# Top-32 mask in a fused attention and MoE kernel: from a compare-multiply-sum on VectorE to a parametric ReLU and an exponential on ScalarE

## The chip, the cores and the metric

The kernel runs on one core of a Trainium2 chip. The metric is the device time of one execution in microseconds (us). Five engines work beside each other, each through its own instructions in a fixed order: PE (matrix multiplication, with its weight loads shown as PEld), DVE (vector), ACT (scalar, activation functions), POOL (GpSimd) and SP (which only issues DMAs here). An engine waits at an instruction until what it needs is there, and everything behind it on that engine waits too.

## The reference

Three layers are computed one after the other, all in float32:

```python
# 1. attention, batch 4, heads 8, sequence 576, head size 64
scores = scale * q @ k.T                       # scale = 1/8
kth = partition(scores, -32)[..., -32]         # the 32nd largest of a row
scores = where(scores >= kth, scores, -1e9)
attn = exp(scores - max(scores))
attn = attn / (sum(attn) + 1e-9)
x = attn @ v                                   # -> 2304 tokens x 512
# 2. h = x @ w_in (512 x 2048);  g = h * cos(h);  x = g @ w_out
# 3. gate: softmax of x @ w_gate (8 experts), 8 Sinkhorn rounds over all tokens
#    out = sum over experts e of P[:, e] * (relu(x @ w1[e]) @ w2[e])   (512 x 1024 x 512 each)
```

## The kernel before

Precision: most products are made of three matmuls on halves ("hi" and "lo") of the float32 operands. ACT makes the hi half as a rounded copy (`split_cols`, L345), POOL or DVE the lo half by a subtraction (L347). Matmuls of that kind stand on lines L372 to L374 and L383 to L387.

Attention works on tiles of 128 query rows by 576 keys. `att_tile` (from L436) makes one of them: PE computes the scores in two halves of 288 columns into one PSUM bank `s` (L447, L448; L451 in the first tiles), ACT copies each half to `sc` (L457). DVE finds the 32 largest values of each row by four MAX8 (L459, L465; each gives eight values, kept in `m`) with three MATCH_REPLACE8 between them (L464), which strike out what was found. The largest value is in column 0 of `m`, the 32nd in column 31. Beside that chain ACT makes the exponentials of all 576 scores (L461), with minus an eighth of the largest value as bias (POOL, L460). When the 32nd value is there, DVE makes one pass (L466) that compares each score with it, multiplies the exponential by the 0 or 1 and sums the row. POOL adds 1e-9 (L468), DVE takes the reciprocal (L469), POOL scales the row (L470), PE turns the tile over by five transposes into PSUM bank `t` (L475), and ACT and DVE split it there into hi and lo (L493, L494). `att_out` (L501 to L509) multiplies by v.

There are 144 such tiles. The first 24 (three query tiles of eight heads, `attention_tile`) come at the start, beside the decoding of the weights `w_in` and `w_out`; they feed the second layer of the first 384 tokens (`moe1_tile_a`, `moe1_tile_b`, L631 to L671). The other 120 (`attention`) come after it. Beside these, PE has filler work: the expert products of the first 384 tokens (`fill(e, 0, LEAD)`, matmuls of 384 and 512 columns), one part of the second layer (`moe1`), and the expert products of the next 512 tokens (`fill(e, LEAD, 4)`). What is left of filler work when attention ends is done after it, then come three more parts of the second layer, the Sinkhorn rounds, and the dense expert products of the remaining tokens.

The order on each engine is not written by hand. `Plan.add` records each operation with its engine, a planned duration and what it reads and writes; `Plan.issue` then walks through a planned time and on each engine takes the ready operation of the best class (`PRIORITY`: on PE attention goes before the filler), and emits the instructions in that order. The planned durations are the second argument of `put`. Changing an operation or its planned duration therefore moves instructions on all engines. Tiles overlap through rings of buffers: four `sc`, two `wk`, three `ex`, four `m`; the PSUM banks `s` and `t` exist once.

Of the kernel before, what the change touches and what calls it, by code (L numbers as in the profile page):

```python
# [14 lines left out]
AF = mybir.ActivationFunctionType  # L15
ALU = mybir.AluOpType
# [5 lines left out]
MAGIC = 12582912.0  # L22
HALF_PI = 1.5707963267948966
LOWEST = -3.0e38


CLASSES = ("first attention", "first mlp", "decode", "attention", "mlp")
# [43 lines left out]
class Plan:  # L71
# [32 lines left out]
    def add(self, eng, cost, emit, reads=(), writes=(), prio=0.0, func=None, nbytes=0):  # L104
        op = Op()
        op.eng, op.cost, op.emit, op.func, op.bytes = eng, cost, emit, func, nbytes
        k = len(self.ops)
        op.prio = (prio, k)
        deps = set()

        def norm(acc):
            for a in acc:
                if isinstance(a, tuple) and isinstance(a[0], View):
                    b, lo, _ = a[0].span
                    yield b, lo + a[1], lo + a[2]
                elif isinstance(a, View):
                    yield a.span
                elif isinstance(a, Buf):
                    yield a, 0, 1 << 30
                else:  # L120
                    yield a

        pools = set()
        for b, lo, hi in norm(reads):
            pools.add(b.pool)
            for l, h, i, wr in b.log:
                if wr and l < hi and lo < h:
                    deps.add(i)
        for b, lo, hi in norm(writes):
            pools.add(b.pool)  # L130
            for l, h, i, wr in b.log:
                if l < hi and lo < h:
                    deps.add(i)
        for b, lo, hi in norm(writes):
            b.log = [e for e in b.log if not (lo <= e[0] and e[1] <= hi)]
            b.log.append((lo, hi, k, True))
        for b, lo, hi in norm(reads):
            b.log.append((lo, hi, k, False))
        for p in pools:
            for old in self.pools[p].get("after", ()):  # L140
                deps.update(self.users.get(old, ()))
                self.users[p + "<"] = True
        for p in pools:
            self.users.setdefault(p, []).append(k)
        deps.discard(k)
        op.deps = deps
        self.ops.append(op)
        return k
# [65 lines left out]
def mm_ns(n):  # L214
    return max(107.0, n / 2.4 + 3.0)


def act_ns(n, psum=False, ap=False):
    return (51.0 if psum else 93.0) + n / 1.2 + (93.0 if ap else 0.0)


def dve_ns(n, fast=False):
    return 66.0 + n * (0.53 if fast else 1.042)
# [6 lines left out]
def fused_kernel(tc, kq, vv, w_in, w_out, w_gate, w1, w2, out, B=4):  # L230
# [4 lines left out]
    V, A_, G_, T_ = nc.vector, nc.scalar, nc.gpsimd, nc.tensor  # L235
    H, S, D = 8, 576, 64
# [25 lines left out]
    def put(eng, cost, emit, reads=(), writes=(), func=None, nbytes=0):  # L262
        return add(eng, cost, emit, reads, writes, PRIORITY[eng][CLASSES.index(work)], func, nbytes)
# [172 lines left out]
    def att_tile(stats, dests, plain=None):  # L436

        at_f = plain and plain["at"]  # L440
        sc, m, wk, ex = sc_r(), m_r(), wk_r(), ex_r()
        for c in (slice(0, 288), slice(288, 576)):
            o = lambda: ps_s.ap[:, 0:288]

            def qk(c=c):
                for i, (q, c0, hd) in enumerate(stats):
                    T_.matmul(o(), q.ap[:, c0 : c0 + 128], hd["kh"].ap[:, c], start=i == 0, stop=False)  # L447
                    T_.matmul(o(), q.ap[:, c0 : c0 + 128], hd["kl"].ap[:, c], start=False, stop=i == len(stats) - 1)  # L448

            def qk_plain(c=c):  # L450
                T_.matmul(o(), plain["q"].ap[:, plain["h"], :], plain["k"].ap[:, plain["h"] % 2, c], start=True, stop=True)  # L451

            if plain:
                put("PE", 4 * mm_ns(288), qk_plain, [plain["q"], plain["k"]], [ps_s])
            else:
                put("PE", 2 * len(stats) * mm_ns(288), qk, [x for q, _, hd in stats for x in (q, hd["kh"], hd["kl"])], [ps_s])
            put("ACT", act_ns(288, psum=True), lambda c=c: A_.activation(sc.ap[:, c], o(), AF.Copy), [ps_s], [(sc, c.start, c.stop)])  # L457
        mc = lambda i, k=1: m.ap[:, i : i + k]
        put("DVE", 669, lambda: V.max(mc(0, 8), sc.ap), [sc], [(m, 0, 8)])  # L459
        put("POOL", 162, lambda: G_.tensor_scalar(mc(32), mc(0), -0.125, 0.0, op0=ALU.mult, op1=ALU.add), [(m, 0, 8)], [(m, 32, 33)])  # L460
        put("ACT", act_ns(S, ap=True), lambda: A_.activation(ex.ap, sc.ap, AF.Exp, scale=0.125, bias=mc(32)), [sc, (m, 32, 33)], [ex], func="exp")  # L461
        for r in range(3):
            src = wk if r else sc
            put("DVE", 669, lambda r=r, src=src: V.match_replace(wk.ap, mc(8 * r, 8), src.ap, LOWEST), [src, (m, 8 * r, 8 * r + 8)], [wk])  # L464
            put("DVE", 669, lambda r=r: V.max(mc(8 * r + 8, 8), wk.ap), [wk], [(m, 8 * r + 8, 8 * r + 16)])  # L465
        put("DVE", 729, lambda: V.scalar_tensor_tensor(ex.ap, sc.ap, mc(31), ex.ap, op0=ALU.is_ge, op1=ALU.mult, accum_out=mc(33)),  # L466
            [sc, ex, (m, 24, 32)], [ex, (m, 33, 34)])
        put("POOL", 162, lambda: G_.tensor_scalar(mc(34), mc(33), 1e-9, 1.0, op0=ALU.add, op1=ALU.mult), [(m, 33, 34)], [(m, 34, 35)])  # L468
        put("DVE", 75, lambda: V.reciprocal(mc(35), mc(34)), [(m, 34, 35)], [(m, 35, 36)])  # L469
        put("POOL", 724, lambda: G_.tensor_scalar(ex.ap, ex.ap, mc(35), 0.0, op0=ALU.mult, op1=ALU.add), [ex, (m, 35, 36)], [ex])  # L470
        pt = lambda: ps_t.ap.rearrange("p (c t) -> p c t", c=4)
        for c0, c1, p in ((0, 4, 128), (4, 5, 64)):
            def tr(c0=c0, c1=c1, p=p):
                for c in range(c0, c1):
                    T_.transpose(pt()[:p, c - c0, :], ex.ap[:, c * 128 : c * 128 + p], ident.ap)  # L475

            put("PE", 109.0 * (c1 - c0), tr, [ex, ident], [ps_t])
            if plain:
                put("ACT", act_ns((c1 - c0) * 128, psum=True), lambda c0=c0, c1=c1, p=p: A_.activation(at_f.ap[:p, c0:c1, :], pt()[:p, 0 : c1 - c0, :], AF.Copy),
                    [ps_t], [(at_f, c0, c1)])  # L480
            for r0, rn, hd, t0 in dests:
                ath, atl = hd["ath"], hd["atl"]
                tv = slice(t0, t0 + rn)
                hv = lambda ath=ath, c0=c0, c1=c1, p=p, tv=tv: ath.ap[:p, c0:c1, tv]
                if c0:

                    lb, lv = ath, lambda ath=ath, tv=tv: ath.ap[64:128, 4:5, tv]
                else:
                    lb, lv = atl, lambda atl=atl, tv=tv: atl.ap[:, :, tv]
                sv = lambda c0=c0, c1=c1, p=p, r0=r0, rn=rn: pt()[:p, 0 : c1 - c0, r0 : r0 + rn]  # L490
                k = (c1 - c0) * rn
                hi, lo = (ath, 1000 * c0 + t0, 1000 * c0 + t0 + rn), (lb, 2000 * c0 + t0, 2000 * c0 + t0 + rn)
                put("ACT", act_ns(k, psum=True), lambda hv=hv, sv=sv: A_.activation(hv(), sv(), AF.Copy), [ps_t], [hi])  # L493
                put("DVE", dve_ns(k), lambda hv=hv, sv=sv, lv=lv: V.tensor_tensor(lv(), sv(), hv().bitcast(F32), op=ALU.subtract), [ps_t, hi], [lo])  # L494
# [602 lines left out]
```

## Time and profile before

| | us |
|---|---|
| device time, median of 3 runs | 2463.03 |
| lowest and highest run | 2460.49, 2464.35 |
| span of the profiled execution | 2460.7 |
| PE busy (matmul), DVE busy | 2367.6, 1997.4 |
| ACT busy, POOL busy | 1274.0, 1291.5 |

Of the profiled execution the page gives the span alone, the time from its first instruction to its last; the runs that were timed without a profile lie from 0.2 us under it to 3.7 us over it, their median 2.3 us over it. A busy PE is not a PE at its peak: the shown end of a matmul contains a latency in which the next ones already run, so the pace of PE is read from how many matmuls start in a stretch.

The span falls into four parts, told apart by what runs in them: the first 24 attention tiles with the decoding (0 to about 246 us), a hand-over in which the second layer of the first tokens is finished (to 289.3 us, where the first filler matmul starts), the 120 attention tiles with filler (to 1280 us, where the last attention matmul ends), and the rest without attention.

### The profile page before, as it was taken

What the parts mean: (1) busy time and instruction counts of PE and PEld (TensorE: products, weight loads), DVE (VectorE), ACT (ScalarE), POOL (GpSimd) and SP (SyncE); (2) the same over time, 40 slices, a digit from 0 to 9 for tenths busy, and PEclk for the clock granted to TensorE, in tenths of its full rate; (3) what the DMA queues carried; (4) which work ended last, traced back from release to release, by engine and by line L of the source; (5) the groups of instructions that cost most, each with busy time, mean ns of one, the idle gap of its engine ahead of it and who ended that gap; (6) DMA issues with size and microseconds to landing.
All of it is one profiled execution on the core that took longest, in us unless ns stands there. A gap on an engine that the chain in (4) does not pass through costs nothing.

```text
span 2460.7 us, 33833 instructions
## 1 busy us (share of the span) xinstructions
PE 2367.6 (96%) x11161; PEld 1907.1 (78%) x11161; DVE 1997.4 (81%) x3659; ACT 1274.0 (52%) x2468; POOL 1291.5 (52%) x1352
## 2 busy tenths in 40 slices
PE   6888899999988999999999999999999999999999
PEld 3444588888876778877788888888888888888887
DVE  8998599999999999999988778776666666666655
ACT  6785566666777656666556776422222223222221
POOL 6886487778876656665530035534333334443330
PEclk9679999999999999999999999999999999999999
DMA  8766654545523333433333333122222211111101
GB/s 266 225 210 198 194 167 142 158 136 174 171 68 98 107 116 117 119 116 100 94 113 115 103 104 118 27 73 84 84 78 77 73 61 35 43 42 36 35 22 48
DMA packets 162449, 267.44 MB, mean 109 GB/s; under 512 B 15392, under 2 KB 62576, under 8 KB 162272
## 3 DMA queue, kind: packets, MB, share of 16 engines
q1 hardware_dynamic: 162272, 265.27, 35.6%
q8 instruction: 88, 1.44, 0.3%
q14 instruction: 89, 0.73, 0.1%
HBM read 233.34 MB, written 31.87 MB: 108 GB/s over the span
## 4 chain that ended last, share of the span: by engine, by line
PE 51%; DVE 27%; POOL 4%; issue 3%; ACT 2%; DMA 1%; POOLq 0%; SPq 0%; ACTq 0%; DVEq 0%
PE y L372 8%; PE y L373 8%; PE y L374 8%; DVE wk L464 7%; DVE m L465 6%; DVE ex L466 4%; DVE atl L494 2%; DVE m L459 2%; DVE gl L761 2%; PE g L374 2%; PE g L373 2%; PE g L372 2%; PE y L387 1%; PE y L384 1%; PE y L383 1%
## 5 line engine op out<-in xcount | busy, mean ns | idle before, releaser
L347 POOL TENSOR_TENSOR wlo<-raw,whi 128x512 fp32r<-128x512 f32 x336 | 453.5, 1354 | 153.1 <-ACT whi L345 110.0
L465 DVE MAX8 m<-wk 128x8 f32<-128x576 f32 x432 | 318.3, 748 | 1.9
L955 DVE SCALAR_TENSOR_TENSOR acc<-y,P,acc 128x512 f32<-128x512 f32 x308 | 228.4, 747 | 98.3 <-PE y L374 98.2
L345 ACT ACTIVATE whi<-raw 128x512 fp32r<-128x512 f32 x416 | 258.7, 627 | 92.2 <-PE y L374 35.9
L464 DVE MATCH_REPLACE8 wk<-m,wk 128x576 f32<-128x576 f32 x288 | 213.6, 742 | 1.5
L372 PE MATMUL y<-whi,gh 128*128 128x512 f32 x448 | 181.9, 406 | 0.0
L374 PE MATMUL y<-whi,gl 128*128 128x512 f32 x448 | 176.4, 394 | 0.0
L372 PE MATMUL y<-gh,xh 128*128 128x512 f32 x450 | 176.1, 391 | 0.1
L373 PE MATMUL y<-wlo,gh 128*128 128x512 f32 x448 | 175.8, 392 | 0.0
L373 PE MATMUL y<-gl,xh 128*128 128x512 f32 x450 | 175.5, 390 | 0.0
L374 PE MATMUL y<-gh,xl 128*128 128x512 f32 x450 | 175.3, 390 | 0.0
L475 PE MATMUL t<-ident,ex 128*128 128x128 f32 (+1 forms) x720 | 136.6, 290 | 34.3 <-POOL ex L470 7.9
L457 ACT ACTIVATE sc<-s 128x288 f32<-128x288 f32 x288 | 117.1, 407 | 95.9 <-DVE ex L466 58.7
L466 DVE SCALAR_TENSOR_TENSOR ex<-sc,m,ex 128x576 f32<-128x576 f32 x144 | 164.5, 1142 | 1.3
L475 PEld LDWEIGHTS t<-ident,ex 128*128 128x128 f32 (+1 forms) x720 | 86.4, 141 | 98.8 <-POOL ex L470 26.0
L461 ACT ACTIVATE ex<-sc,m 128x576 f32<-128x576 f32 x144 | 111.4, 774 | 45.3 <-POOL m L460 44.3
L493 ACT ACTIVATE ath<-t 64x128 fp32r<-64x128 f32 (+3 forms) x272 | 104.9, 397 | 54.8 <-PE t L475 48.5
L470 POOL TENSOR_SCALAR ex<-ex,m 128x576 f32<-128x576 f32 x144 | 111.2, 772 | 38.2 <-DVE m L469 37.1
L459 DVE MAX8 m<-sc 128x8 f32<-128x576 f32 x144 | 107.0, 743 | 8.9 <-ACT sc L457 8.8
L464 DVE MATCH_REPLACE8 wk<-m,sc 128x576 f32<-128x576 f32 x144 | 106.6, 740 | 0.0
L372 PEld LDWEIGHTS y<-gh,xh 128*128 128x128 f32 x450 | 84.5, 188 | 19.1 <-DVE acc L951 0.7
L372 PE MATMUL y<-gh,gh 128*128 128x512 f32 x254 | 99.2, 391 | 0.0
(376 smaller groups left out, 7109.2 us busy)
## 6 DMA issues: line engine op xcount, KB each, us to landing
raw<-in_w_dram SPq DMA_DIRECT2D x384, 256.0 KB, 2.7
kq<-in_kq_dram SPq DMA_DIRECT2D x40, 576.0 KB, 4.0
raw<-win_d SPq DMA_DIRECT2D x64, 256.0 KB, 3.0
raw<-wout_d SPq DMA_DIRECT2D x64, 256.0 KB, 2.7
y_d<-st SPq DMA_DIRECT2D x56, 256.0 KB, 3.1
raw<-y_d SPq DMA_DIRECT2D x56, 256.0 KB, 2.7
wp<-win_d SPq DMA_DIRECT2D x24, 512.0 KB, 4.7
wp<-wout_d SPq DMA_DIRECT2D x24, 512.0 KB, 4.1
```

The source lines that it names most:

```text
L345: put("ACT", act_ns(n), lambda: A_.activation(hv(), rv(), AF.Copy), [rb], [hb])
L347: put(e, c, lambda: f.tensor_tensor(lv(), rv(), hv().bitcast(F32), op=ALU.subtract), [rb, hb], [lb])
L372: T_.matmul(o(), ah(), bh(), start=start, stop=False)
L373: T_.matmul(o(), ah(), bl(), start=False, stop=False)
L374: T_.matmul(o(), al(), bh(), start=False, stop=stop)
L457: put("ACT", act_ns(288, psum=True), lambda c=c: A_.activation(sc.ap[:, c], o(), AF.Copy), [ps_s], [(sc, c.start, c.stop)])
L459: put("DVE", 669, lambda: V.max(mc(0, 8), sc.ap), [sc], [(m, 0, 8)])
L464: put("DVE", 669, lambda r=r, src=src: V.match_replace(wk.ap, mc(8 * r, 8), src.ap, LOWEST), [src, (m, 8 * r, 8 * r + 8)], [wk])
L465: put("DVE", 669, lambda r=r: V.max(mc(8 * r + 8, 8), wk.ap), [wk], [(m, 8 * r + 8, 8 * r + 16)])
L466: put("DVE", 729, lambda: V.scalar_tensor_tensor(ex.ap, sc.ap, mc(31), ex.ap, op0=ALU.is_ge, op1=ALU.mult, accum_out=mc(33)), [sc, ex, (m, ...
L475: T_.transpose(pt()[:p, c - c0, :], ex.ap[:, c * 128 : c * 128 + p], ident.ap)
L955: put("DVE", 663, lambda y=y, av=av, pcol=pcol: V.scalar_tensor_tensor(av(), y.ap, pcol(), av(), op0=ALU.mult, op1=ALU.add), [y, P, a], [a])
```

## The change

The compare-multiply-sum pass on DVE goes. The exponential is made after the 32nd value is known, by two ACT instructions in a row. The first is a parametric ReLU of (32nd value minus score): where the score is under the 32nd value the argument is positive and stays as it is, where it is not the argument is multiplied by 2^-100. The second is an exponential of that, scaled by minus an eighth of 2^100, with an eighth of (32nd value minus largest value) as bias, and it also gives the sum of the row: a kept score comes out as before, and all others as exp of a huge negative number, which is zero. The bias is made by POOL with the same kind of instruction as before, but from two columns of `m`, and so not before the 32nd value.

```diff
@@ -22,6 +22,7 @@
+TINY = 2.0**-100
@@ -457,14 +458,14 @@
         mc = lambda i, k=1: m.ap[:, i : i + k]
         put("DVE", 669, lambda: V.max(mc(0, 8), sc.ap), [sc], [(m, 0, 8)])
-        put("POOL", 162, lambda: G_.tensor_scalar(mc(32), mc(0), -0.125, 0.0, op0=ALU.mult, op1=ALU.add), [(m, 0, 8)], [(m, 32, 33)])
-        put("ACT", act_ns(S, ap=True), lambda: A_.activation(ex.ap, sc.ap, AF.Exp, scale=0.125, bias=mc(32)), [sc, (m, 32, 33)], [ex], func="exp")
         for r in range(3):
             ...
-        put("DVE", 729, lambda: V.scalar_tensor_tensor(ex.ap, sc.ap, mc(31), ex.ap, op0=ALU.is_ge, op1=ALU.mult, accum_out=mc(33)),
-            [sc, ex, (m, 24, 32)], [ex, (m, 33, 34)])
+        put("POOL", 162, lambda: G_.tensor_scalar(mc(32), mc(31), mc(0), 0.125, op0=ALU.subtract, op1=ALU.mult), [(m, 0, 8), (m, 24, 32)], [(m, 32, 33)])
+        put("ACT", act_ns(S, ap=True), lambda: A_.activation(ex.ap, sc.ap, AF.Prelu, scale=-1.0, bias=mc(31), alpha=TINY), [sc, (m, 24, 32)], [ex])
+        put("ACT", act_ns(S, ap=True) + 93.0, lambda: A_.activation(ex.ap, ex.ap, AF.Exp, scale=-0.125 / TINY, bias=mc(32), accum_out=mc(33)),
+            [ex, (m, 32, 33)], [ex, (m, 33, 34)], func="exp")
         put("POOL", 162, lambda: G_.tensor_scalar(mc(34), mc(33), 1e-9, 1.0, op0=ALU.add, op1=ALU.mult), [(m, 33, 34)], [(m, 34, 35)])
```

The emitted order moves on every engine. Three places follow. Line numbers of the changed kernel are higher by one up to L459 and from L467 on (L466 is the parametric ReLU there, L467 the exponential, L463 and L464 are MATCH_REPLACE8 and the later MAX8).

DVE, in the middle of the 120 attention tiles, from the last MAX8 of one tile (`m_169`) to its reciprocal, before; `gl` is filler, `ath` and `atl` are the lo halves of other tiles:

```order
L465 MAX m_169<-wk_183 128x8
L761 SCALAR_TENSOR_TENSOR gl_1951<-g,gh_1937 128x384
L494 TENSOR_TENSOR ath_1581<-t,ath_1581 64x64
L494 TENSOR_TENSOR ath_1696<-t,ath_1696 64x64
L466 SCALAR_TENSOR_TENSOR ex_137,m_169<-sc_151,m_169,ex_137 128x576
L465 MAX m_200<-wk_134 128x8
L469 RECIPROCAL m_169<-m_169 128x1
```

The same place on DVE after the change, for the tile whose values are in `m_167`; `x` is an output of attention:

```order
L464 MAX m_167<-wk_188 128x8
L464 MAX m_195<-wk_134 128x8
L460 MAX m_248<-sc_208 128x8
L463 MATCH_REPLACE wk_134<-m_195,wk_134 128x576
L510 TENSOR_TENSOR x_1810<-t,avt_1804 64x192
L464 MAX m_195<-wk_134 128x8
L463 MATCH_REPLACE wk_188<-m_248,sc_208 128x576
L463 MATCH_REPLACE wk_134<-m_195,wk_134 128x576
L470 RECIPROCAL m_167<-m_167 128x1
```

The pass over `ex` is gone, and the reciprocal, which needs the sum of the row, now stands behind seven instructions of other tiles. Over the 120 tiles the middle value is seven instructions between the two; the smallest values are none (twice).

ACT around the same two tiles, before (the exponential of `m_169`'s tile, `ex_137`) and after (the two instructions on `ex_278`):

```order
L457 ACTIVATE sc_213<-s 128x288
L345 ACTIVATE kh_1383<-kq_117 128x576
L345 ACTIVATE whi_1721<-raw_139 128x512
L461 ACTIVATE ex_137<-sc_151,m_169 128x576
L493 ACTIVATE ath_1696<-t 128x4x128
L790 ACTIVATE st_1444<-y_754 128x512
```

```order
L346 ACTIVATE kh_1452<-kq_122 128x576
L466 ACTIVATE ex_278<-sc_138,m_167 128x576
L509 ACTIVATE avt_1804<-t 64x192
L346 ACTIVATE whi_1721<-raw_132 128x512
L346 ACTIVATE vs_1449<-vraw_120 128x5x64
L467 ACTIVATE ex_278,m_167<-ex_278,m_167 128x576
L431 ACTIVATE qt_1438<-kq_122 128x64
L458 ACTIVATE sc_138<-s 128x288
```

The parametric ReLU waits for the tile's last MAX8, and copies for other tiles and for the filler stand behind it. In most tiles, as here or directly behind each other, the exponential follows within a few instructions. Over the whole program ACT has 2587 ACTIVATE where it had 2443, and 23 table loads (ACT_TABLE_LOAD) where it had 25; none of the 23 stands in front of a parametric ReLU.

PE at the end of attention, where the last product with v (`vs`) stands, before and after:

```order
L374 MATMUL h<-xh,wlo_1741 128x512
L501 MATMUL t<-ath_1696,vs_1414 128x320
L503 MATMUL t<-atl_1700,vs_1414 128x320
```

```order
L375 MATMUL h<-x2fh,wlo_1787 128x512
L502 MATMUL t<-ath_1640,vs_1459 128x320
L504 MATMUL t<-atl_1647,vs_1459 128x320
```

Before, the expert fillers (products with `x2fh`) were all done by then and the next part of the second layer (`xh`) had begun; after, expert fillers are still under way. Counted over the order, 4992 matmuls stand from the first filler matmul to the last attention matmul before, and 4613 after: 379 filler matmuls, most of 512 columns, have moved behind attention.

## Rows read from the trace of the kernel before

**Rows 1.** Windows of the whole core: busy us (instructions) per engine, granted clock, DMA.

```profile
core 0: us, PE busy (x) PEld busy (x) DVE busy (x) ACT busy (x) POOL busy (x), PEclk, DMA share, GB/s
0.00:246.00 246.00, 199.69 (x637) 99.58 (x638) 222.36 (x425) 171.55 (x328) 184.11 (x199) 0.83 0.72 225
246.00:289.30 43.30, 37.90 (x133) 19.24 (x132) 14.68 (x27) 19.81 (x36) 12.15 (x14) 0.99 0.67 218
...
289.30:1280.00 990.70, 956.56 (x4995) 796.30 (x4994) 962.17 (x2032) 650.58 (x1368) 678.20 (x797) 0.99 0.42 126
...
1353.00:1414.50 61.50, 61.50 (x272) 49.86 (x271) 45.84 (x65) 43.65 (x70) 5.96 (x4) 1.00 0.34 104
```

**Rows 2.** Groups by line, 289.3 to 1280 us: count, busy us, mean ns, idle before.

```profile
L465 DVE MAX8 m<-wk 128x8 f32<-128x576 f32 x351 | 259.1, 749 | 1.8
...
L466 DVE SCALAR_TENSOR_TENSOR ex<-sc,m,ex 128x576 f32<-128x576 f32 x117 | 132.6, 1133 | 1.1
...
L457 ACT ACTIVATE sc<-s 128x288 f32<-128x288 f32 x232 | 94.7, 408 | 77.0 <-DVE ex L466 53.1 <-PE s L448 19.9 <-PE y L374 1.8
...
L461 ACT ACTIVATE ex<-sc,m 128x576 f32<-128x576 f32 x117 | 90.6, 774 | 38.5 <-POOL m L460 37.5
...
L761 DVE SCALAR_TENSOR_TENSOR gl<-g,gh 128x384 fp32r<-128x384 f32 (+1 forms) x64 | 39.1, 611 | 0.2 <-ACT gh L760 0.2
```

**Rows 3.** The removed pass, whole span: shortest, middle, longest ns; who waited for it.

```profile
L466 DVE SCALAR_TENSOR_TENSOR ex<-sc,m,ex x144: 792/924/1975, 18.9 to 1265.8; 128x576 f32<-128x576 f32 x144
...
  POOL m L468: 91.4, 83
  ACT sc L457: 58.7, 58
```

**Rows 4.** Timeline around one such pass: start us, length us.

```profile
1131.78 1.30 POOL L347 TENSOR_TENSOR wlo<-raw,whi 128x512 fp32r<-128x512 f32 x1 [2.10 <-PE t L503]
...
1132.13 1.57 DVE L466 SCALAR_TENSOR_TENSOR ex<-sc,m,ex 128x576 f32<-128x576 f32 x1
...
1133.63 0.08 DVE L466 DVE_READ_ACCUMULATOR ex<-sc,m,ex 128x1 f32 x1
1133.63 0.47 DVE L509 TENSOR_TENSOR x<-t,avt 64x320 f32<-64x320 f32 x1
```

**Rows 5.** Groups of PE by line and shape, 289.3 to 1280 us.

```profile
L372 PE MATMUL y<-whi,gh 128*128 128x512 f32 x448 | 181.9, 406 | 0.0
...
L475 PE MATMUL t<-ident,ex 128*128 128x128 f32 x468 | 72.5, 277 | 12.4 <-POOL ex L470 5.8 <-DVE x L509 3.0 <-DVE ath L494 2.6
L447 PE MATMUL s<-kh,qs 128*128 128x288 f32 x202 | 67.7, 335 | 4.3 <-ACT sc L457 4.1
...
L372 PE MATMUL h<-x2fh,whi 128*128 128x512 f32 x128 | 52.6, 411 | 0.0
...
L372 PE MATMUL g<-x2fh,whi 128*128 128x384 f32 x128 | 45.3, 354 | 0.0
```

**Rows 6.** Timeline of PE: pitch of matmuls of 288 and 384 columns.

```profile
310.11 0.30 PE L447 MATMUL s<-kh,qs 128*128 128x288 f32 x1
310.25 0.29 PE L448 MATMUL s<-kl,qs 128*128 128x288 f32 x1
310.38 0.34 PE L372 MATMUL h<-x2fh,whi 128*128 128x384 f32 x1
...
311.43 0.30 PE L447 MATMUL s<-kh,qt 128*128 128x288 f32 x1
```

**Rows 7.** Groups by line, 0 to 246 us.

```profile
L466 DVE SCALAR_TENSOR_TENSOR ex<-sc,m,ex 128x576 f32<-128x576 f32 x26 | 31.1, 1198 | 0.1
```

**Rows 8.** Groups of ACT over the whole span: nearest to what is added.

```profile
L345 ACT ACTIVATE kh<-kq 128x576 fp32r<-128x576 f32 x40 | 27.2, 680 | 0.0
...
L594 ACT ACT_TABLE_LOAD x12 | 15.4, 1283 | 0.2
```

## The prediction

> **What bounds the kernel now.** First read the busy time stage by stage, not over the span. In the 990.7 us in which the 120 attention tiles run, DVE is busy 962.2 us, 97%; ACT is busy 66% and POOL 68% [rows 1]. 117 of the 144 passes that go stand there. Beside each, DVE has seven others over 576 columns, MAX8 and MATCH_REPLACE8, of some 0.75 us each: a queue that hardly ever runs empty [rows 2]. What the changed instruction delays is read from the idle time in front of others: copies of new scores to SBUF (L457) waited 53.1 us for it, since they overwrite what it reads [rows 2], and POOL's next step (L468) 91.4 us over the whole span [rows 3].
>
> PE is shown as busy 956.6 us in the same stretch, but that is not its pace. Count instead. Where there is no attention, 272 matmuls of 512 columns fit in 61.5 us, 0.226 us each [rows 1]. Those of 384 columns start 0.175 us apart (six from 310.38 to 311.43), those of 288 columns 0.135 us [rows 6]. In the stretch there are 1344 matmuls of 512 columns on `y` (three lines of 448), 768 on `h` and `g`, and some 430 of the second layer: 2542 x 0.226 = 574 us. 768 of 384 columns (six groups of 128) make 134 us. The 524 for scores, 586 transposes and 576 products with v are small ones, which I put at 0.12 us each, a little under the 288-column pitch: 1686 x 0.12 = 202 us [rows 5, 6]. Together PE needs 911 us of the 990.7, so it stands still for 80 us in all, in many short waits. That is the most that relief of DVE can give back in this stretch, since filler work that attention does not cover has to be done behind it at PE's full pace.
>
> Before 246 us DVE is busy 222.4 us, 90%, with 26 of the passes; PE has little to do there and POOL and ACT are at 75% and 70%. From 246 to 289 us nothing is at its limit (DVE 14.7 of 43.3 us): that is the chain of the last second-layer tile [rows 1]. The rest of the span has none of the changed work.
>
> **The change part by part.**
>
> *The pass that goes.* 117 passes at 1.133 us mean [rows 2]. Its shown end overlaps the next instruction: the pass that starts at 1132.13 for 1.57 us is followed at 1133.63, 0.07 us earlier than its end; the reading of its sum starts together with the next instruction and costs nothing [rows 4]. So 117 x (1.133 - 0.07) = 124 us of DVE. The spread says why it is that long: 0.79 us at the shortest, 1.98 at the longest [rows 3]. The one shown began while POOL ran a subtraction of two SBUF operands until 1133.08, and ended 0.6 us after that, as if it had waited for it [rows 4]. So a third of the saving is a wait between DVE and POOL, and it goes with the pass.
>
> *Filler that moves.* By the order, 379 filler matmuls leave the stretch, nearly all of 512 columns: 379 x 0.226 = 86 us of PE that comes back behind attention at full price. With every 24 of them one DVE pass L761 leaves (0.61 us): 16 x 0.61 = 10 us.
>
> *What DVE and PE need then.* DVE 962 - 124 - 10 = 828 us; PE 911 - 86 = 825 us. They meet, so one is no longer covered by the other. DVE's idle time of before was 990.7 - 962.2 = 28.5 us; I keep it, and add 10 us, because two engines that are both full and run in a fixed order wait for each other more often. The stretch lasts 828 + 28 + 10 = 866 us, and 86 us follow: 952 against 991, a gain of 39. Ends: both engines wait 5 us in all: 833 + 86 = 919, a gain of 72; or PE's 80 us of waits all stay: 825 + 80 + 86 = 991, no gain.
>
> *The first 24 tiles.* 26 passes of 1.198 us fall before 246 us [rows 7]: 26 x (1.198 - 0.07) = 29 us of DVE. DVE is 90% busy, but decoding also runs through POOL and ACT, and ACT gets the added work. Bounds: all 29 us or none; half of it, 15 us, is taken. The hand-over of 43 us then starts earlier and stays as it is.
>
> *ACT's added work.* The exponential exists in both kernels; it has a bias from a column and takes 0.774 us [rows 2]. The parametric ReLU is not in the trace. The nearest rows bound it: a rounded copy of 576 columns takes 0.680 us [rows 8], the exponential of 576 with its bias column 0.774; it has such a column too, so 0.774 is taken. Reading the sum I put at 0.08 us, as on DVE [rows 4]. 117 x 0.85 = 100 us more for ACT in the stretch, less about 27 us of copies that leave with the filler (16 times three copies of some 0.56 us): 651 + 73 = 724 us of 866, 84%. That is not the bound, and I cost it at nothing; its cover is the 16% idle time of ACT. In the first 246 us ACT goes from 171.6 to 194 of 231 us, also 84%.
>
> *The longer chain.* From the last MAX8 to the reciprocal there were one pass on DVE and a POOL step; now there are the parametric ReLU, the exponential and the POOL step, some 1.9 us and the hand-offs. On DVE seven instructions of other tiles stand in between, mostly of 0.6 to 0.75 us, some 4 us: that covers it, but for the few tiles where fewer stand there. In ACT's queue the copies for the filler (`whi`, `gh`) and for scores wait behind the parametric ReLU, which waits for DVE; the copies of scores lose in exchange the 53.1 us in which they waited for the pass [rows 2]. POOL's bias step changes its inputs, not its length.
>
> A rule weighed against the rows: a parametric ReLU is here the work of a compare, and on ACT it takes 0.774 us by the row next to it, while the DVE pass takes 0.79 us when it waits for nobody [rows 3]: by duration alone nothing is won. The Trainium skill, "ScalarE: Activation LUTs", section "Rules for kernel authors", says to put relu and mul on VectorE and not on ScalarE; by it the change goes the wrong way, and if duration on the engine decided, it would cost 144 x (0.85 - 0.79) = 9 us. The rows decide otherwise, because one engine is 97% busy and the other 66%.
>
> **Sum.** 39 + 15 = 54 us from the profiled span of 2460.7: 2407 us. The runs' median lies 2.3 us above that span, so about 2409 us.
>
> **Rivals.**
>
> *Full relief*: both engines fill the stretch (gain 72) and DVE sets the first 246 us (29): 2463 - 101 = 2362 us. For it: DVE idles hardly at all before, except for 28 us; the POOL waits shrink too. Against it: both are full at once, and the first 246 us also lean on POOL.
>
> *PE's waits stay*: the 80 us are not DVE's fullness but the order in which PE meets transposes and products that aren't ready; the chain is now longer by one ACT pass. For it: transposes waited for the scaled row and for DVE's split alike [rows 5]. Against it: those are ends of DVE's chain. The stretch gives nothing, the start 15: 2448 us.
>
> *ACT holds up the others (slower)*: the parametric ReLU stands at the head of ACT's queue until DVE delivers, and filler copies, score copies and splits behind it start late, so that DVE and PE both idle. For it: copies already waited for POOL or DVE 53.1 and 37.5 us [rows 2]. The gain of 54 us is eaten when every one of the 144 tiles adds 0.37 us of idle time; if each of the 117 tiles in the stretch adds one ACT pass of 0.77 us, that is 90 us, and the time is 2409 + 90 = 2499 us. Against it: the score copies waited for the same DVE chain before.
>
> *Table loads*: if the parametric ReLU were not in the table that holds the exponential, each tile would load two, 288 x 1.283 = 370 us of ACT [rows 8], which would then need more than the stretch has: some 250 us slower, 2710 us. The order shows no load in front of it, 23 in all. The Trainium skill, "ScalarE: Activation LUTs", section "Table sets: the hidden batching unit", says that cheap functions are in every set, without naming this one; by that rule there is no load either.
>
> **How the numbers follow.** Forecast 0.52 (its own range 2380 to 2440), full relief 0.17, PE's waits stay 0.17, ACT holds up 0.13, table loads 0.01. From low to high: the range 2360 to 2452 leaves out the slow cases and a part of the outer edges, some 0.2. What this kernel's measurements can tell from no change is 0.2%, 5 us. Faster by more: the forecast, full relief and two thirds of the third case, 0.81; within: 0.06, the third case where the start gives nothing either; slower: the last two, 0.14 less a rounding, 0.13.
>
> **What would show it.** Right: the line L466 of before is gone on DVE; tiles follow each other every 866 / 117 = 7.4 us instead of 990.7 / 117 = 8.5; DVE is still over 90% busy in the stretch and PE's pace there comes nearer to its pace behind attention; ACT between 80 and 88%; reciprocals wait under 0.2 us per tile; more expert fillers behind attention; POOL's subtractions get shorter, as they no longer meet the pass. Wrong: DVE idle before the reciprocal or before the first MAX8 by half a microsecond and more per tile, on ACT; the parametric ReLU over 1 us; table loads beside it; a first filler matmul no earlier than 289 us.

## The result and the profile after

The changed kernel takes 2428.9 us (median of four runs, 2426.9 to 2435.1) where the one before takes 2463.7 on the same chip: ratio 0.9866, 95% interval 0.9851 to 0.9882. Predicted were 2409 us, a range of 2360 to 2452 and faster with a chance of 0.81. So sign and range held: 35 of the 54 us of gain came, 19 are missing. The profiled execution is the slowest of its runs, 6 us over their median: its span is 2433.3 us, 27.4 under that of before, so the profile shows 7 us less gain than the medians do. Every profile here is one execution, and runs of one kernel lie up to 10 us apart (2455.4 to 2465.7 in experiment 2); in which part of the span they differ no run shows. A few us between the stretches of two profiles prove nothing by themselves.

The windows of the changed kernel, over the same four parts (the columns are those of [rows 1]; the first filler matmul starts at 298.2 us, the last attention matmul at 1163.6, in the kernel before at 1279.8):

```profile
0.00:246.00 246.00, 189.17 (x604) 95.27 (x604) 175.45 (x349) 183.23 (x365) 174.10 (x190) 0.86 0.69 217
246.00:298.20 52.20, 44.85 (x164) 22.96 (x163) 26.10 (x46) 26.02 (x50) 15.98 (x21) 1.00 0.64 210
298.20:1163.60 865.40, 848.08 (x4614) 726.15 (x4613) 819.58 (x1776) 694.08 (x1543) 643.16 (x772) 1.00 0.44 131
1163.60:1238.00 74.40, 74.40 (x325) 60.67 (x324) 10.16 (x15) 27.23 (x47) 36.37 (x29) 1.00 0.41 118
```

Set against [rows 1], the attention stretch lasts 865.4 us where 866 were predicted (990.4 before, counted likewise to the start of the last attention matmul), with DVE busy 819.6 us (828 predicted) and idle 46 (38 predicted). Behind attention PE runs filler without a pause: 325 matmuls in 74.4 us are 0.229 us each. From the last attention matmul to the end it is 1269.7 us (2433.3 - 1163.6), 88.8 more than before (2460.7 - 1279.8); 86 were predicted. So the stretch with its tail gained 125 - 89 = 36 us, nearly the 39 of the sum. The start went the other way: the first filler matmul comes at 298.2 instead of 289.3 us, 9 us later, where 15 us earlier were predicted. Of the 26.6 us that the profile is short of the forecast, 24 stand there and 3 in the stretch.

The lines that answer to [rows 2], in the stretch of the changed kernel (count, busy us, mean ns, idle time before and what ended it):

```profile
L458 ACT ACTIVATE sc<-s 128x288 f32<-128x288 f32 x233 | 94.4, 405 | 14.0 <-PE s L449 12.2
L467 ACT ACTIVATE ex<-ex,m 128x576 f32<-128x576 f32 x117 | 90.4, 773 | 5.2 <-POOL m L465 2.3
L466 ACT ACTIVATE ex<-sc,m 128x576 f32<-128x576 f32 x117 | 90.3, 772 | 24.0 <-DVE m L464 23.8
...
L467 ACT ACTIVATION_READ_ACCUMULATOR ex<-ex,m 128x1 f32 x117 | 22.2, 190 | 0.0
L470 DVE RECIPROCAL m<-m 128x1 f32<-128x1 f32 x117 | 17.9, 153 | 9.6 <-POOL m L469 8.5
```

The parametric ReLU takes 0.772 us, as the exponential does. Reading the sum is shown as 0.190 us, but it starts before the exponential's shown end and the next instruction starts before its own. Two lines of ACT's timeline (start us, length us):

```profile
900.14 0.78 ACT L467 ACTIVATE ex<-ex,m 128x576 f32<-128x576 f32 x1
...
900.92 0.27 ACT L494 ACTIVATE ath<-t 64x128 fp32r<-64x128 f32 x1
```

The next instruction starts 0.78 us after the exponential. In the kernel before, where no sum is read, it is 0.68 us (446.47 to 447.15 us). So the sum costs ACT about 0.1 us per tile, near the 0.08 of the prediction. The longer chain hardly shows on DVE: reciprocals waited 9.6 us in all, 0.08 us per tile. The copies of scores hardly wait for DVE any more (14.0 us of idle time before L458, 12.2 of them for PE, in place of the 77.0 of [rows 2]).

What happened in the start is seen in three views of it. First, when the decoding and the tiles are done (POOL's last step of each of the 32 blocks, then ACT's last copy of each of the 24 tiles; shortest, middle, longest ns, then first and last start), before:

```profile
L333 POOL TENSOR_TENSOR d_low<-d_mag,d_low x32: 1262/1272/2366, 21.2 to 211.2; 128x512 f32<-128x512 f32 x32
...
L534 ACT ACTIVATE x_f<-t x24: 252/269/273, 30.7 to 238.4; 64x128 f32<-64x128 f32 x24
```

and after:

```profile
L334 POOL TENSOR_TENSOR d_low<-d_mag,d_low x32: 1257/1268/2298, 19.3 to 231.6; 128x512 f32<-128x512 f32 x32
...
L535 ACT ACTIVATE x_f<-t x24: 254/268/279, 32.3 to 202.7; 64x128 f32<-64x128 f32 x24
```

The tiles end 36 us earlier, but the last weights are decoded 20 us later. Before, tiles were last; now decoding is. Second, the window from 185 to 246 us, before and after, where the engines fall idle:

```profile
185.00:246.00 61.00, 52.50 (x213) 28.12 (x214) 54.70 (x105) 34.40 (x69) 40.81 (x49) 0.97 0.61 198
```

```profile
185.00:246.00 61.00, 37.17 (x85) 16.70 (x85) 18.58 (x22) 32.50 (x62) 49.86 (x45) 0.75 0.71 235
```

DVE falls from 54.7 to 18.6 us: its tiles are done, and it idles while POOL, busy 49.9 us, works off the decoding. (PE's granted clock falls there too, from 0.97 to 0.75, a mean of its two levels; what that costs no run separates.) The chain of work that ended last, followed back from 300 us, runs through this decoding from 188 to 230 us, and from its last step through the reading back of the weights to PE (start us, length us; two of its pieces):

```profile
228.66 1.23 POOL d_low L334
...
237.59 6.14 DMA wp<-wout_d
```

Third, the waits of the changed kernel, of POOL (0 to 230 us) and of PE (140 to 300 us; total us, times, longest):

```profile
POOL m L469 <- ACT ex L467: 20.5, 9, 6.2
POOL d_mag L331 <- ACT d_mag L330: 20.1, 6, 13.6
```

```profile
PE y L657 <- DMA wp<-wout_d: 15.4, 6, 6.4
```

POOL waits for the new exponential's sum with decoding queued behind it, and the second layer's last matmuls wait for `w_out`, which is read back only after it is decoded. Both waits shrink in the faster starts of experiments 6 to 8: the first to 7 to 10 us, the second to 0.9 us, 7.1 us and nothing. POOL's other wait, for ACT inside the decoding, does not (22 to 25 us there), so it isn't what was lost.

### The profile page after: what moved, and what is told of

It is laid out like the page before. It is cut to its first block, busy times and chain, and to the rows that moved or that the text cites. A ratio compares the mean times of both kernels' runs of the same rounds, so it can differ in the third digit from the quotient of the medians.

```text
span 2433.3 us, 33804 instructions
## 1 busy us (share of the span) xinstructions
PE 2344.6 (96%) x11161; PEld 1909.7 (78%) x11161; DVE 1835.7 (75%) x3371; ACT 1370.4 (56%) x2754; POOL 1285.8 (53%) x1352
## 4 chain that ended last, share of the span: by engine, by line
PE 77%; DVE 10%; POOL 5%; ACT 3%; DMA 3%; issue 2%; SPq 0%; POOLq 0%; ACTq 0%; DVEq 0%
PE y L373 11%; PE y L374 11%; PE y L375 11%; PE g L375 3%; PE g L374 3%; PE g L373 3%; PE t L476 2%; DVE wk L463 2%; PE h L373 2%; PE h L374 2%; PE h L375 2%; DVE m L464 2%; PE t L502 1%; PE y L385 1%; PE y L384 1%
## 5 line engine op out<-in xcount | busy, mean ns | idle before, releaser
L348 POOL TENSOR_TENSOR wlo<-raw,whi 128x512 fp32r<-128x512 f32 x336 | 448.6, 1340 | 144.6 <-ACT whi L346 110.2
L464 DVE MAX8 m<-wk 128x8 f32<-128x576 f32 x432 | 317.4, 748 | 2.8
L463 DVE MATCH_REPLACE8 wk<-m,wk 128x576 f32<-128x576 f32 x288 | 213.9, 743 | 1.8
L458 ACT ACTIVATE sc<-s 128x288 f32<-128x288 f32 x288 | 116.5, 405 | 26.0 <-PE s L449 12.9
L466 ACT ACTIVATE ex<-sc,m 128x576 f32<-128x576 f32 x144 | 111.0, 771 | 33.1 <-DVE m L464 32.9
L467 ACT ACTIVATE ex<-ex,m 128x576 f32<-128x576 f32 x144 | 111.2, 772 | 5.5 <-POOL m L465 2.3
L463 DVE MATCH_REPLACE8 wk<-m,sc 128x576 f32<-128x576 f32 x144 | 106.7, 741 | 0.2
```

Source lines behind the costliest of these rows:

```text
L348: put(e, c, lambda: f.tensor_tensor(lv(), rv(), hv().bitcast(F32), op=ALU.subtract), [rb, hb], [lb])
L467: put("ACT", act_ns(S, ap=True) + 93.0, lambda: A_.activation(ex.ap, ex.ap, AF.Exp, scale=-0.125 / TINY, bias=mc(32), accum_out=mc(33)), [ ...
```

## The experiments

All use the two kernels' code with the edit shown. For each, the time is the median, the ratio that to the kernel before on the same chip; times of different experiments can come from different chips, and there the ratios are the better comparison. A table of where the start ended in every profile comes after them.

**1. The old form in the first 24 tiles, the new in the other 120.**

```diff
+        old = plain
+        if old:
             ...  # bias, exponential as before
-        put("DVE", 729, ...)
+        if old:
+            put("DVE", 729, ...)
+        else:
+            ...  # bias, Prelu, Exp as in the change
```

> Old form in the first 24 tiles, new form in the other 120. Theory A (the start is lost because ScalarE's added work goes ahead of the weight decoding in the plan, so the decoding ends late): the first filler matmul is back at 289 us (298 in the changed kernel, 289 in the one before), the attention stretch keeps its gain, time 2463 - 39 = 2424 us or a little under. Rival B (the first filler matmul moves for a reason that has nothing to do with the first 24 tiles, such as what the plan does with the later ones): it stays near 298 us and the time near 2429.

2422.4 us, ratio 0.9834 (0.9819 to 0.9848): faster than the whole change. The first filler matmul is back at 286.1 us, and the stretch keeps its gain: it lasts 885.5 us, with 101 matmuls more than in the change, which at 0.226 us make 23 us. The start's loss comes with the new form of the first 24 tiles.

**2. The new form in the first 24 tiles alone** (the condition turned round).

> New form in the first 24 tiles only, old form in the other 120; the decoding stands as in the changed kernel (21 of 32 blocks before the 24th tile is scaled). All theories that blame the start: first filler matmul at 296 to 300 us and the stretch as before, so 2463 + 9 = 2472 us, slower than before. If the start isn't to blame: 2450 to 2463.

2459.1 us, ratio 0.9989 (0.9978 to 0.9999). The first filler matmul comes at 300.4 us, as expected of the start. The time was missed: 2472 us were expected, and 2459 lies where the theory that the start isn't to blame put it. The stretch was not as before: the order changed there too and holds 77 matmuls more (5072 against 4995 in the windows). 77 x 0.226 = 17 us of filler were taken in, while it grew by 997.9 - 990.4 = 7.5 us. So in the profile the start costs 11 us and the order of the rest gives 10 back; this run doesn't price the start by itself.

**3. The pass cut to 8 of 576 columns, order unchanged.**

```diff
-V.scalar_tensor_tensor(ex.ap, sc.ap, mc(31), ex.ap, op0=ALU.is_ge, ...
+V.scalar_tensor_tensor(ex.ap[:, :8], sc.ap[:, :8], mc(31), ex.ap[:, :8], op0=ALU.is_ge, ...
-... G_.tensor_scalar(mc(34), mc(33), 1e-9, 1.0, ...
+... G_.tensor_scalar(mc(34), mc(33), 1e3, 1.0, ...
```

> The kernel before with its order unchanged; the pass is cut to 8 of 576 columns, so there is no mask and the sum is not that of the row (a constant of 1000 is added to it). No work is added to ScalarE. Theory (VectorE is the bound, then TensorE at 911 us of need): the attention stretch goes from 991 to 930 to 945 us, the start ends 15 to 29 us earlier (first filler matmul at 260 to 274 us), time about 2390 us. Rival (TensorE's 80 us of waits come from the order and not from VectorE): the stretch stays over 970 us, time over 2430.

2417.8 us, ratio 0.9813 (0.9797 to 0.9829). The first filler matmul comes at 275.6 us, 14 us earlier (15 to 29 were expected): that is what this relief of DVE is worth in the start, with the order kept. The time lies 28 us over the 2390 that were expected. The stretch, and the cut pass over the whole span and in the stretch:

```profile
275.60:1228.20 952.60, 937.75 (x4992) 799.26 (x4992) 900.33 (x2032) 648.90 (x1368) 658.64 (x798) 1.00 0.42 131
```

```profile
L466 DVE SCALAR_TENSOR_TENSOR ex<-sc,m,ex x144: 203/365/1411, 18.6 to 1214.6; 128x8 f32<-128x8 f32 x144
...
L466 DVE SCALAR_TENSOR_TENSOR ex<-sc,m,ex 128x8 f32<-128x8 f32 x117 | 62.9, 538 | 1.1
```

952.6 us, 7 over the forecast's upper end: DVE fell only from 962 to 900 us, since a pass of 8 columns takes 0.20 us at the shortest, but 0.54 us on average in the stretch and up to 1.41. The stretch gained 38 us with no work added to ACT, hardly more than the 36 of the change. The rival, over 970 us, fell. PE's waits, counted by the prediction's estimate of its need, were 80 us and are 42 here (952.6 - 911) and 40 in the changed kernel (865.4 - 825): by this count the gain ends where PE becomes the bound too.

**4. ACT's added work without its wait, order unchanged.**

```diff
+        def two():
+            A_.activation(ex.ap, sc.ap, AF.Prelu, scale=-1.0, bias=mc(32), alpha=TINY, accum_out=mc(36))
+            A_.activation(ex.ap, sc.ap, AF.Exp, scale=0.125, bias=mc(32))
-        put("ACT", act_ns(S, ap=True), lambda: A_.activation(ex.ap, sc.ap, AF.Exp, ...
+        put("ACT", act_ns(S, ap=True), two, ...
```

> The kernel before with its order unchanged; in front of each exponential ScalarE makes a parametric ReLU of the same size with a sum, which nobody uses: the change's added ScalarE work (some 0.77 + 0.19 us a tile by the changed kernel's trace) without its wait for the 32nd value. Theory (ScalarE's 34% idle time covers it): within 0.4% of before, at most 10 us longer, first filler matmul at 289 to 295 us. Rival (ScalarE's load itself holds up others): 25 us longer and more, of which the start has 9 or more.

2507.9 us, ratio 1.0182 (1.0165 to 1.0199). The rival was right (its 9 us in the start were 8), and with it a step of the prediction falls. The stretch:

```profile
297.30:1323.80 1026.50, 968.78 (x4992) 789.21 (x4992) 964.43 (x2032) 743.22 (x1602) 679.06 (x797) 1.00 0.40 121
```

ACT is busy 743 of 1026.5 us, 72%, and the stretch is 36 us longer, 0.31 us per tile. An engine with a quarter of its time idle was not a cover. The likely reason is that its work stands in one queue, and an instruction that the plan did not count on delays all behind it. The transposes then waited longer for DVE's splits, and those for ACT's:

```profile
PEld t L480 <- DVE atl L499: 32.6, 55, 2.9
```

(15.8 us before; the splits' own wait for ACT in front of them rose from 2.4 to 18.5 us). In the start the added work cost 8 us (297.3). In the change the plan knows of the work and moves other work, and DVE has the pass no more; which of the two makes the difference no run separates, since DVE here is as full as before. That the work costs nothing in the change was not shown, only that the stretch as a whole came out as summed.

**5. Decoding before the tiles on ACT, the change otherwise.**

```diff
-    "ACT": (0, 0.5, 1, 2, 1.5),
+    "ACT": (1, 0.5, 0, 2, 1.5),
```

> The changed kernel with one edit: on ScalarE the decoding of the weights goes before the first attention tiles in the plan (classes 0 and 1 exchanged). By the order all 32 blocks are decoded before the 16th tile is scaled (21 of 32 before the 24th in the changed kernel). Theory A: the first filler matmul comes at 265 to 285 us instead of 298, time 2400 to 2418 us. Rival B (it is the longer chain of each tile that costs the start, not the order of the decoding): the first filler matmul stays at 295 us or later, time 2425 or more.

2450.4 us, ratio 0.9948 (0.9933 to 0.9962): 21 us slower than the change. Decoding ended at 181.6 us, 50 earlier, but the last tile at 268.0, 65 later, and the first filler matmul came at 314.3. My theory in this form was wrong, and rival B's figures came, although experiment 6 speaks against its cause. It isn't that decoding has to be first: here the tiles were late instead, and the hand-over needs both.

**6. The change with the plan of before in the start.** Only the planned duration of one instruction is changed, so the work is that of the change.

```diff
-            put("DVE", 669, lambda r=r: V.max(mc(8 * r + 8, 8), wk.ap), ...
+            put("DVE", 669 + 729 * bool(plain and r == 2), lambda r=r: V.max(mc(8 * r + 8, 8), wk.ap), ...
```

> The changed kernel; only the planned duration of the last MAX8 of the first 24 tiles is 729 ns longer, as if the removed pass were still there, so that the plan again puts decoding between these tiles as before (30 of 32 blocks before the 24th tile is scaled, 21 in the changed kernel, 32 in the one before; filler in the attention stretch nearly as in the changed kernel). The work is that of the changed kernel. Theory C (the start is lost by the order alone: the plan, seeing VectorE free, sends the tiles ahead and leaves decoding for the end): first filler matmul at 275 to 288 us instead of 298, time 2408 to 2420 us. Rival D (it is lost by ScalarE's added load and the longer chain, whatever the order): first filler matmul at 292 us or later, time 2424 or more.

2419.8 us, ratio 0.9824 (0.9806 to 0.9842). First filler matmul at 283.9 us, 14 earlier than in the change with the same instructions, and the interval of the ratio lies wholly under that of the change (0.9851 to 0.9882): the start's loss was the order. Of the 14 us some 10 reach the time.

**7. and 8. The same with 400 and with 1000 ns.**

> As the run with 729 ns, with 400 ns more on the planned duration of the last MAX8 of the first 24 tiles: 26 of 32 blocks are decoded before the 24th tile is scaled. Theory C (the start hangs on how far decoding is by then: 21 blocks gave 298 us, 30 gave 284): first filler matmul at about 290 us, between the two; time 2420 to 2430. Rival (that the 729 run gained by chance of the order): anything outside 285 to 297.

2416.4 us, ratio 0.9809 (0.9795 to 0.9824); first filler matmul at 285.4 us, 5 earlier than the 290 expected, time under the range.

> The same with 1000 ns: all 32 blocks are decoded before the 24th tile is scaled, 24 before the 16th. Theory C: the gain levels off, since the tiles now come as late as decoding: first filler matmul at 280 to 287 us, time 2412 to 2424. With all blocks before the 16th tile it was 314. Rival: a further gain of the same size (first filler matmul under 278), or a loss (over 290).

2415.6 us, ratio 0.9811 (0.9794 to 0.9829); first filler matmul at 275.6 us. A levelling off was expected; the rival, a further gain, came in the start. In the time it is hardly seen: this profile is the fastest of its runs and the change's the slowest, 24.7 us apart, the medians 13. The start ends where that of experiment 3 does, which has no work added to ACT at all: in this order the added work shows no cost there, though the two orders differ, and the equality to a tenth of a us is chance. Decoding and the tiles end 14 us apart here (212.9 and 226.8 us).

By their medians the runs with 400, 729 and 1000 ns are some 9 to 13 us faster than the change, and the intervals of their ratios lie under the change's; among each other they overlap.

**9. Measured durations for MAX8 and MATCH_REPLACE8 in the plan.**

```diff
-        put("DVE", 669, lambda: V.max(...        # first and later MAX8
+        put("DVE", 685, lambda: V.max(...
-            put("DVE", 669, lambda r=r, src=src: V.match_replace(...
+            put("DVE", 742, lambda r=r, src=src: V.match_replace(...
```

> The changed kernel with the planned durations of MAX8 and MATCH_REPLACE8 as the trace has them (685 and 742 ns instead of 669): the order changes on all engines, 25 of 32 blocks are decoded before the 24th tile is scaled, and 4828 matmuls stand from the first filler matmul to the last attention matmul (4612 in the changed kernel). Theory C: the start gains in part (first filler matmul at 285 to 296 us), and TensorE is the bound in the attention stretch, so its waits there stay at about what they are: time 2415 to 2430. Rival (the waits in the stretch come from planned durations that are too short): they fall, time under 2410.

2430.6 us, ratio 0.9874 (0.9859 to 0.9888), no better than the change and 0.6 us over the range. The start ended at 289.9 us, in the range; the 8 us of it are not seen in the median. 218 filler matmuls, 49 us of PE, moved back into the stretch, which grew by 913.8 - 865.4 = 48 us: PE is the bound there, while DVE is busy 846 us of it, and truer durations didn't shorten its waits.

**10. New form in half of the first 24 tiles.**

```diff
-        old = plain
+        old = plain and plain["h"] % 2
```

> New form in the 120 later tiles and in the first tiles of the four even heads; old form in the first tiles of the odd heads. Half of the removed passes and half of ScalarE's added work in the start, 30 of 32 blocks decoded before the 24th tile is scaled. Theory C: first filler matmul at 275 to 288 us, time 2408 to 2422. Rival D: half way between 286 (all old) and 298 (all new), 292 us, time about 2426.

2426.8 us, ratio 0.9856 (0.9842 to 0.9871), first filler matmul at 290.0 us: theory C's ranges were missed, by 2 us in the start and 5 in the time, though 30 of 32 blocks stand before the 24th tile. Rival D's figures, 292 and about 2426, came closer; but its cause, load and chain whatever the order, can't be the whole, since experiments 6 to 8 start earlier with all of that load. The count of blocks was the wrong measure; the time at which decoding ends (226.7 us) goes better with the start, as the table shows.

The end of the decoding and of the last tile in each profile, and the first filler matmul (us). The last column is the later of (decoding + 65) and (tile + 50). Both offsets were fitted to these rows, so it describes them, to within 4 us, and predicts nothing:

| | decoding | last tile | first filler | later of the two |
|---|---|---|---|---|
| before | 211.2 | 238.4 | 289.3 | 288.4 |
| change | 231.6 | 202.7 | 298.2 | 296.6 |
| 1 old form in the start | 211.4 | 237.7 | 286.1 | 287.7 |
| 2 new form in the start alone | 234.6 | 205.7 | 300.4 | 299.6 |
| 3 pass of 8 columns | 200.1 | 225.6 | 275.6 | 275.6 |
| 4 ACT's work added | 214.3 | 246.0 | 297.3 | 296.0 |
| 5 decoding first on ACT | 181.6 | 268.0 | 314.3 | 318.0 |
| 6 plan + 729 ns | 218.4 | 219.3 | 283.9 | 283.4 |
| 7 plan + 400 ns | 223.8 | 214.7 | 285.4 | 288.8 |
| 8 plan + 1000 ns | 212.9 | 226.8 | 275.6 | 277.9 |
| 9 measured durations | 226.5 | 208.6 | 289.9 | 291.5 |
| 10 new form in half | 226.7 | 228.3 | 290.0 | 291.7 |

## Why the prediction held in one half and not in the other

*What bounds the stretch* held. DVE was the bound, and with the pass gone DVE and PE met: 820 us of DVE and, by the estimate of its need, 825 of PE in 865. Experiment 9 shows PE as the next bound: 49 us of matmuls more made it 48 us longer. One of the two largest rivals, that PE's waits stay, fell: 80 us became 40 by the same estimate.

*The pass* was sized nearly right. DVE's busy time fell by 143 us: 124 and 10 were summed. A third of the pass was put down to a wait for POOL, and that holds: over the shortest pass, 117 x (1.133 - 0.792) = 40 us were spent before, and with 8 columns still 117 x (0.538 - 0.203) = 39 us. POOL's side of it was mis-sized. Its subtractions in the stretch, before and after:

```profile
L347 POOL TENSOR_TENSOR wlo<-raw,whi 128x512 fp32r<-128x512 f32 x285 | 382.9, 1346 | 136.3 <-ACT whi L345 93.3 <-issue 20.7 <-PE t L475 4.8
```

```profile
L348 POOL TENSOR_TENSOR wlo<-raw,whi 128x512 fp32r<-128x512 f32 x263 | 350.1, 1335 | 94.5 <-ACT whi L346 60.1 <-issue 10.9 <-POOL m L465 4.7
```

1.346 and 1.335 us: they hardly got shorter. POOL did wait where a pass began just before its subtraction, as here in the kernel before (start us, length us):

```profile
618.87 0.81 DVE L466 SCALAR_TENSOR_TENSOR ex<-sc,m,ex 128x576 f32<-128x576 f32 x1
618.93 1.91 POOL L347 TENSOR_TENSOR wlo<-raw,whi 128x512 fp32r<-128x512 f32 x1
```

But that was so for some 20 of the 285; DVE did most of the waiting.

*Filler that moves* held: 86 us summed, 89 measured.

*ACT's added work at no cost* was argued from idle time and is not a valid step: experiment 4 prices the same work at 36 us in the stretch where the order isn't made for it and DVE is full. That the sum of the stretch came out is in part luck: the plan had moved other work, 10 us of extra waiting had been allowed, and ACT was busy 694 us where 724 were summed. The added work takes 743 - 651 = 93 us of ACT in experiment 4 (100 summed), so some 49 us of its other work left the stretch, not 27. The 37.5 us that the rival on ACT names were a wait of the exponentials for POOL, not of copies.

*The first 24 tiles* is the step that failed: "half of it, 15 us, is taken", with 0 and 29 us as bounds, and a loss was not among them. DVE's relief is worth 14 us there (experiment 3). What was missed is that the plan sees the relief as well. Two chains must end before the hand-over, tiles and decoding; the plan lets the tiles go first on ACT and POOL, and with DVE free they left the decoding behind, whose end moved from 211 to 232 us. The difference between the change and experiment 6, the same work in another order, is 14.3 us; ACT's added work in an order not made for it cost 8.0 (experiment 4). -13.7 + 8.0 + 14.3 = +8.6, measured +8.9. That these add up so well is luck: they are single executions in three orders, and experiment 8 shows no such 8 us. The number to see it by stood in the emitted order before any run: 32 of 32 blocks decoded when the 24th tile is scaled before, 21 after. I read the order in the stretch and not in the start.

The parametric ReLU takes 0.77 us on ACT and the pass 0.79 us at its shortest on DVE, and the kernel is 1.3% faster. The rule weighed in the prediction, to keep relu and mul on VectorE (the Trainium skill, "ScalarE: Activation LUTs", section "Rules for kernel authors"), did not decide here. No table load stands in front of a parametric ReLU, 23 in all, as the order had said.

## What to carry to other kernels

When a planner orders the work, a shorter operation moves everything that competes with its successors: for every stretch, compare in the new order what must be finished at its end, not only what stands next to the edit. Where two chains must both end before the next stage, relief of one can make the other late, and a planned duration is a cheap handle to set the balance (9 to 13 us here, experiments 6 to 8). Idle time of an engine is no proof that added work is covered: 34% were not enough in experiment 4.

## What the runs showed of the hardware

A DVE instruction with two SBUF operands took 0.79 us at the shortest and up to 1.98 beside a POOL subtraction of two SBUF operands [rows 3, 4]. The same form on 8 columns took 0.20 to 1.41 us (experiment 3), with as much time over the shortest in all (39 us against 40), so the wait does not shrink with the size. It goes both ways: the POOL subtraction that began 0.06 us after a pass took 1.91 us, where they average 1.35. The Trainium skill, "SBUF — State Buffer", section "SBUF: two separate sides", speaks of a shared port pair that the one that starts first holds for its whole instruction; both waits agree with that. An ACT instruction that also gives the sum of its rows is followed by a reading that is shown as 0.19 us but overlaps its neighbours, and adds about 0.1 us (0.78 us to the next start against 0.68); on DVE the reading is shown as 0.08 us and starts together with the next instruction [rows 4].
